# Sigmoid attention and a skip MoE: each block's kind read inside the block before, and the gathers' index tiles made one step earlier

## The chip, the core and the metric

The kernel runs on one core of a Trainium2 chip. A core has five engines with an instruction stream each: TensorE (PE in the profile; its weight loads are shown apart as PEld), VectorE (DVE), ScalarE (ACT), GpSimd (POOL) and SyncE (SP), which here issues transfers. An engine has a sequencer, which reads the stream, runs register operations, branches and waits itself, and hands the rest to the engine. The profile marks what a sequencer does with a q (PEldq, DVEq, ...). They meet only through semaphores. The metric is the device time of one execution in microseconds, lower is better.

## The reference

Inputs are `q`, `k`, `v` of shape (8, 12, 448, 64) and the weights of a mixture of 8 experts (768 to 1024 to 768), all float32.

```python
scores = scale * q @ k.T - log(448)
attn = sigmoid(scores)                      # no softmax: each weight by itself
x = (attn @ v) as 3584 rows of 768
do_compute = (x @ w_skip) > 0               # other rows pass through unchanged
e = argmax(x @ w_gate); gate = probability of e
out[row] = x[row] + gate * (relu(x[row] @ w1[e]) @ w2[e])
```

So each row that isn't skipped goes to one expert, and how many rows an expert gets is known only at run time.

## The kernel before

The attention takes the first part of the span (to about 284 us). It writes `x` to the output in DRAM, and for every row a record (gate, row number) to a list in DRAM, sorted by expert. The experts' weights are 6.3 MB each in float32, so they are streamed.

Two full blocks of 128 rows of the first expert are computed in straight code while the planner works out the rest: a table `slots` (line 1085) with three entries for each block that is to come. `HAS` says whether a further expert's weights are to be loaded, `NXT` which one, and `TYP` the kind of the block. Then a loop (line 1537) runs over the remaining blocks; its count is a register. In the profiled execution it turns 14 times. There are four kinds, each an arm of a nested branch (`choose`, line 1525; the branches are shown at lines 1526, 1527 and 1532):

- FULL (0) and SPLIT (3), both by `block`: 128 rows. A float32 product is made of three faster ones of high and low parts. SPLIT also takes the next expert's weights apart into such parts: high parts on ACT (`hi1`, `hi2`), low parts on DVE (`lo1`, `lo2`).
- HALF (2) and FEW (1): the remaining rows of an expert, at most 64 or 32 of them, multiplied with the raw float32 weights. The few rows leave most of PE's columns free, so two or four parts of a product run side by side. These arms also issue the loads of the next expert's weights on SP.

In the profiled execution a full-size block and a HALF or FEW block alternate: full, HALF, full, HALF, then full and FEW five times. The last FEW block ends the kernel.

Inside an arm the order of each engine's work is the order in the source (`manual_schedule` in `run`, line 1520). The parts that the change touches are:

- The loop's head, line 1538: `kind = entry(TYP, ds(i + 2, 1), mybir.ALL_ENGINES, SPLIT)`. All five engines load one word of `slots` from SBUF into a register (`entry`, line 1088; the loads appear at line 1089, as do the loads of `NXT` and `HAS` on SP). Then each engine branches by it. The limits given to a load are checked by a SEQ_ASSERT instruction.
- `fetch` (line 1262), once in each arm, behind the transposes `turn_x` (line 488, shown at 492) that empty `xn`. On POOL it touches `xn` and `rn`, makes the index tiles (`jk`, `ri`, `rx`, `rp[1]`, `rq`) from the record `rn` and the list of slots `rix`, and issues two gathers: the rows of the block after the next into `xn`, and the records of the one behind that into `rn`.
- `put` (line 1285), at the end of each arm. On POOL it copies the row numbers, waits for the finished rows (`seen`), copies them to `ys` in FULL and FEW arms, and scatters them with addition into the output.
- `shift` (line 1278): DVE moves the list `rix` on by one block, between `fetch` and `put`.
- `ready_x` (line 1105): ACT and DVE turn the transposed rows of the next block into `xh`, `xf` and `xl`. `take_rec`, `weigh_sum` and `advance` (DVE) handle the gates and row numbers.

In a FEW arm PE's order is: first layer (96 small matmuls into `ph`), transpose of the first half of the hidden rows (line 1412), `turn_x` (six transposes), transpose of the second half (line 1416), second layer (32 small matmuls into `py`). Both halves come from ACT (line 1408), and go back through ACT (line 1419).

Of the kernel before, what the change touches and what calls it, by code (L numbers as in the profile page):

```python
# [15 lines left out]
ALU = mybir.AluOpType  # L16
# [7 lines left out]
def kernel(  # L24
# [11 lines left out]
    nc = tc.nc  # L36
# [487 lines left out]
    def relu(h, hs, ph):  # L524
        nc.scalar.activation(hs[:, h * H1 : (h + 1) * H1], ph[h], AF.Relu)  # L525
# [683 lines left out]
    def next_expert(col):  # L1209
        return entry(NXT, col, SP, NE - 1), entry(HAS, col, SP, 1)  # L1210
# [30 lines left out]

    dve, pool = nc.vector, nc.gpsimd

    order.__exit__(None, None, None)
# [16 lines left out]

    def fetch():


        pool.tensor_tensor(xn[:, 0:1], xn[:, 0:1], zf, op=ALU.add)
        pool.tensor_tensor(jk, rn[:, 0:2], rn[:, 0:2], op=ALU.add)
        pool.tensor_copy(ri, rn[:, 1:2])
        pool.tensor_tensor(rn[:, 0:1], rn[:, 0:1], zf, op=ALU.add)
        pool.tensor_tensor(rx, rix[:, 5:6], zero, op=ALU.add)
        pool.tensor_tensor(rp[1], ri, zero, op=ALU.add)  # L1270
        pool.tensor_tensor(rq, rp[1], zero, op=ALU.add)
        got = gather(xn, rp[1])

        tc.declare_no_dep(got.ins, group="put", across_iterations=True, reason="a token is in one block only")
        tc.add_to_no_dep_group("got", got.ins)
        gather_rec(rn, rx)
# [8 lines left out]
    def put(n, last=None):  # L1285

        pool.tensor_tensor(rp[0], rid[:, 0:1], zero, op=ALU.add)
        pool.tensor_tensor(rs, rp[0], zero, op=ALU.add)
        if last is False:
            pool.drain()  # L1290
# [17 lines left out]
        tc.declare_no_dep(out_rows.ins, group="got", across_iterations=True, reason="a token is in one block only")  # L1308
        tc.add_to_no_dep_group("put", out_rows.ins)

    def advance(pieces=2):
# [15 lines left out]
    def block(i, last):  # L1327


        def split1(js, h):  # L1330
            if last:
                for j in js:
                    hi1(j, h)
                for j in js:
                    lo1(j, h)

        gemm1(0, range(G1), xh, xl, ph, last)
        relu(0, hs, ph)
# [6 lines left out]
        gemm1(1, range(9, G1), xh, xl, ph, last)  # L1345
        relu(1, hs, ph)
        for h in range(2):
            turn_x(xn, h, pxt[h])
        fetch()
        split1(range(3), 1)  # L1350
        gemm2(0, hh, hl, py)
# [3 lines left out]
        if last:  # L1355
            for h in range(2):
                whole_x(h, (slice(0, 3),))
            shift(dve)
        else:
            ready_x()  # L1360
        for j in range(1, NK2):
            gemm2(j, hh, hl, py)
# [11 lines left out]
        else:  # L1374
            shift(dve)
        for o in range(2):
            rows = ys if last else yt
            weigh_sum(rows[:, o * H2 : (o + 1) * H2], half_y(py, o), recs[:, 0, 0:1])
# [6 lines left out]
    def few(i):  # L1385

        nx = next_expert(ds(i + 2, 1))
        take_rec()

# [23 lines left out]
        for h in range(2):  # L1413
            turn_x(xn, h, pxt[h])
        fetch()
        nc.tensor.transpose(turned[1][:, :P], hs[:, parts[1]], ident)
        ht4 = ht[:, : 8 * SM].rearrange("p (c g t) -> p c g t", c=2, g=4)
        for s, p in zip(parts, turned):
            nc.scalar.activation(ht[:, s], p[:, :P], AF.Copy)
        ready_x()  # L1420
        shift(dve)

        for n, j in enumerate((0, 2, 1, 3)):
# [28 lines left out]
    def half(i):  # L1452

        nx = next_expert(ds(i + 2, 1))
        take_rec()

# [20 lines left out]
        for h in range(2):  # L1477
            turn_x(xn, h, pxt[h])
        fetch()
        for c in range(4):  # L1480
# [7 lines left out]
        ready_x()  # L1488
        shift(dve)

        ht8 = ht.rearrange("p (c h t) -> p c h t", c=4, h=2)
# [33 lines left out]
    def choose(kind, i):  # L1525
# [5 lines left out]
        with c.Else():  # L1531
            with tc.If(kind < SPLIT) as d:
                run(HALF, i)
            with d.Else():
                run(SPLIT, i)

    with tc.For_i(0, nreg, 1, iteration_sync="reg_based") as i:
        kind = entry(TYP, ds(i + 2, 1), mybir.ALL_ENGINES, SPLIT)
        choose(kind, i)
# [28 lines left out]
```

## Time and profile before

| | |
|---|---|
| median of 3 runs | 526.78 us (526.13 to 526.92) |
| the profiled execution's own time | 526.53 us |
| its span | 524.8 us |
| mean granted TensorE clock | 0.995 |
| busy share of the span: PE, DVE, ACT, POOL | 97%, 56%, 54%, 50% |
| loop, first matmul to the end of the span | 323.7 to 524.8 us |

How to read it: the span goes from the first to the last instruction of the program that the profile shows; the execution's own time has a little more around it. A row of instructions gives a line, an engine, an operation, what is written and read, and a count. In a timeline a row begins with the start and the duration in us, and brackets hold the engine's idle time before the instruction and what ended it; an idle time of POOL ahead of an operation that waits for a later engine costs nothing. Rows with three numbers between slashes give the shortest, the median and the longest duration in ns, then the first and last start in us. In the list of waits a row gives the total in us, how often, and the longest.

### The profile page before, as it was taken

What the parts mean: (1) busy time and instruction counts of PE and PEld (TensorE: products, weight loads), DVE (VectorE), ACT (ScalarE), POOL (GpSimd) and SP (SyncE); (2) the same over time, 40 slices, a digit from 0 to 9 for tenths busy, and PEclk for the clock granted to TensorE, in tenths of its full rate; (3) what the DMA queues carried; (4) which work ended last, traced back from release to release, by engine and by line L of the source; (5) the groups of instructions that cost most, each with busy time, mean ns of one, the idle gap of its engine ahead of it and who ended that gap; (6) DMA issues with size and microseconds to landing.
All of it is one profiled execution on the core that took longest, in us unless ns stands there. A gap on an engine that the chain in (4) does not pass through costs nothing.

```text
span 524.8 us, 15310 instructions
## 1 busy us (share of the span) xinstructions
PE 508.7 (97%) x5033; PEld 339.2 (65%) x5034; DVE 296.1 (56%) x721; ACT 281.0 (54%) x485; POOL 262.5 (50%) x414
## 2 busy tenths in 40 slices
PE   8999999999999999999989999999999999999991
PEld 7765555545545456555445989948669797978790
DVE  4556757648667676687684962862222322269422
ACT  5776776767767668677664211942112323268322
POOL 4523553443557666766574332553333645455644
PEclk9999999999999999999999999999999999999997
DMA  8999787898999999999955023979393959695942
GB/s 211 209 257 200 150 187 156 178 175 173 195 206 234 220 203 221 196 204 213 199 105 114 11 92 105 389 210 347 99 364 119 317 230 310 240 328 227 346 184 47
DMA packets 140288, 107.21 MB, mean 204 GB/s; under 512 B 97099, under 2 KB 112731, under 8 KB 140240
## 3 DMA queue, kind: packets, MB, share of 16 engines
q1 hardware_dynamic: 134000, 97.66, 70.0%
q0 software_dynamic: 4576, 8.65, 6.9%
q8 instruction: 30, 0.49, 0.4%
q10 hardware_dynamic: 1664, 0.26, 0.3%
q14 instruction: 18, 0.15, 0.1%
HBM read 98.49 MB, written 17.56 MB: 221 GB/s over the span
## 4 chain that ended last, share of the span: by engine, by line
PE 89%; DVE 3%; SPq 2%; DMA 2%; issue 1%; ACT 1%; POOL 0%; POOLq 0%; ACTq 0%; DVEq 0%
PE s L212 23%; PE pa L240 21%; PE ph L516 11%; PE py L544 11%; PE b_ph L516 3%; PE b_py L544 3%; PE ph L1391 3%; PE py L1458 2%; PE ph L1458 2%; PE pxt L492 2%; PE py L1391 2%; PE pl L280 1%; PE pht L530 1%; DMA out_dram<-y 1%; SPq L263 1%
## 5 line engine op out<-in xcount | busy, mean ns | idle before, releaser
L232 ACT ACTIVATE at<-s,bias 128x896 f32<-128x896 f32 (+1 forms) x191 | 173.3, 913 | 82.1 <-PE s L212 71.2
L212 PE MATMUL s<-x 64*64 64x448 f32 (+1 forms) x1528 | 165.4, 498 | 1.3 <-DVE wh L485 0.9
L240 PE MATMUL pa<-at,v 64*64 64x448 f32 (+1 forms) x1536 | 163.0, 489 | 0.0
L176 POOL COPY kq<-kq 32x896 f32<-32x896 f32 (+1 forms) x96 | 88.1, 917 | 94.6 <-DMA kq<-in_q_dram 59.0
L212 PEld LDWEIGHTS s<-x 64*64 64x64 f32 x1528 | 80.0, 191 | 53.1 <-issue 28.6
L240 PEld LDWEIGHTS pa<-at,v 64*64 64x64 f32 x1536 | 62.5, 133 | 54.9 <-issue 47.8
L194 DVE STREAM_TRANSPOSE x<-kq 128x448 f32<-128x448 f32 x94 | 80.8, 934 | 5.0 <-POOL kq L176 5.0
L250 DVE TENSOR_TENSOR xt<-xt,pa 128x448 f32<-128x448 f32 x48 | 29.7, 620 | 54.4 <-ACT xt L673 49.6
L414 POOL DMA_INDIRECT lst<-rec,idx x32 | 31.7, 989 | 17.4 <-DVE xt L250 5.8
L486 POOL TENSOR_TENSOR wl<-wr,wh 128x384 fp32r<-128x384 f32 (+1 forms) x28 | 31.2, 1125 | 12.6 <-DVE wh L485 8.1
L255 DVE STREAM_TRANSPOSE y<-xt 128x448 f32<-128x448 f32 x48 | 31.0, 645 | 6.8 <-DMA out_dram<-y 5.2
L574 POOL DMA_INDIRECT out_dram<-ys,rp x15 | 23.7, 1580 | 16.6 <-issue 8.4
L525 ACT ACTIVATE hs<-ph 128x512 f32<-128x512 f32 x14 | 8.3, 596 | 43.9 <-PE ph L516 37.5
L536 DVE TENSOR_TENSOR hl<-pht,hh 128x512 fp32r<-128x512 f32 x14 | 9.7, 690 | 36.5 <-ACT hh L535 22.8
L544 PE MATMUL py<-wh,hh 128*128 128x384 f32 x112 | 29.8, 347 | 0.0
L502 DVE TENSOR_TENSOR xl<-pxt,xh 128x384 fp32r<-128x384 f32 x30 | 15.3, 552 | 25.3 <-ACT xf L1097 17.8
L544 PE MATMUL py<-wh,hl 128*128 128x384 f32 x112 | 28.8, 338 | 0.0
L544 PE MATMUL py<-wl,hh 128*128 128x384 f32 x112 | 28.7, 337 | 0.0
L516 PE MATMUL ph<-wh,xh 128*128 128x512 f32 x84 | 25.7, 402 | 1.1 <-ACT yt L1444 0.8
L516 PE MATMUL ph<-wl,xh 128*128 128x512 f32 x84 | 26.6, 403 | 0.0
L673 ACT ACTIVATE xt<-pa 128x448 f32<-128x448 f32 x48 | 25.7, 536 | 0.8 <-PE pa L240 0.8
L516 PE MATMUL ph<-wh,xl 128*128 128x512 f32 x84 | 24.5, 395 | 0.0
(277 smaller groups left out, 686.4 us busy)
## 6 DMA issues: line engine op xcount, KB each, us to landing
raw<-in_moe_w_dram SPq DMA_DIRECT2D x64, 768.0 KB
v<-in_v_dram SPq DMA_DIRECT2D x48, 256.0 KB
out_dram<-y SPq DMA_DIRECT2D x192, 56.0 KB
kq<-in_k_dram SPq DMA_DIRECT2D x46, 224.0 KB
kq<-in_q_dram SPq DMA_DIRECT2D x46, 224.0 KB
wr<-in_moe_w_dram SPq DMA_DIRECT2D x12, 256.0 KB
wr<-in_moe_w_dram SPq DMA_DIRECT2D x16, 192.0 KB
lst<-fill SPq DMA_DIRECT2D x4, 464.0 KB
```

Of the source, the lines that this page charges most:

```text
L176: nc.gpsimd.tensor_copy(a[BT:, :, :, :BT], a[:BT, :, :, BT:])
L194: nc.vector.transpose(xs[:, n].rearrange("p (r j) -> p j r", j=NJ), t.rearrange("p (j d) -> p j d", d=D)[:, :, :BT],)
L212: nc.tensor.matmul(sc[m * D : (m + 1) * D, j, : qs.stop - qs.start], xs[r, 0, first::NR7], xs[r, 1, qs], start=True, stop=True,)
L232: nc.scalar.activation(at[:, :, :n], sc[:, :, :n], AF.Sigmoid, bias=bias, scale=SCALE)
L240: nc.tensor.matmul(pa[j * D : (j + 1) * D, r, qs], vt[rs, j, r + c if c < 3 else 3 * (1 - r), :], at[rs, j, : qs.stop - qs.start], start=( ...
L250: nc.vector.tensor_tensor(x, x, pa[:, 1, :S], op=ALU.add)
L255: nc.vector.transpose(y, xts[b][:, hp, :])
L414: put = nc.gpsimd.indirect_dma_start(out=lst[:, :], out_offset=bass.IndirectOffsetOnAxis(ap=idx[:, c : c + 1], axis=0), in_=rec[:, c, :], ...
L486: nc.gpsimd.tensor_tensor(lo, r, hi, op=ALU.subtract)
L516: nc.tensor.matmul(ph[h], a[:, j * P : (j + 1) * P], w[j][h], start=(n == 0), stop=(n == len(t) - 1),)
L544: last = nc.tensor.matmul(half_y(py, o), a[h][:, js], w[j][:, o * H2 : (o + 1) * H2], start=(j == 0 and n == 0), stop=(j == NK2 - 1 and n ...
L1391: nc.tensor.matmul(dst[g * SM : (g + 1) * SM, :n], a, w, start=(j == 0), stop=(j == most - 1), tile_position=(0, g * SM),)
```

## The change

The load of the kind leaves the loop's head. Five registers (`kinds`, one for each engine) are filled before the loop, and each arm loads the kind of the next block (`ds(i + 3, 1)`) into them, engine by engine, at places of its own. The loop's head only copies them into the value that the branches compare.

The five POOL operations that make the index tiles leave `fetch` and become `name_rows`. It is called once before the loop, and in `put`: behind the row numbers in FULL, SPLIT and HALF arms, behind the scatter in FEW arms. What remains of `fetch` touches `rn` first and then `xn`. In HALF arms POOL's load of the kind stands inside `fetch`.

```diff
+    ET = mybir.EngineType
+    kinds = nc.alloc_registers("kind", engines=mybir.ALL_ENGINES)
+
+    def next_kind(i, *engines):
+        for e in engines:
+            nc.engines[e].reg_mov(kinds[e], entry(TYP, ds(i + 3, 1), [e], SPLIT))
...
-    def fetch():
-        pool.tensor_tensor(xn[:, 0:1], xn[:, 0:1], zf, op=ALU.add)
+    def name_rows():
         pool.tensor_tensor(jk, rn[:, 0:2], rn[:, 0:2], op=ALU.add)
         pool.tensor_copy(ri, rn[:, 1:2])
-        pool.tensor_tensor(rn[:, 0:1], rn[:, 0:1], zf, op=ALU.add)
         pool.tensor_tensor(rx, rix[:, 5:6], zero, op=ALU.add)
         pool.tensor_tensor(rp[1], ri, zero, op=ALU.add)
         pool.tensor_tensor(rq, rp[1], zero, op=ALU.add)
+
+    def fetch(i=None):
+        pool.tensor_tensor(rn[:, 0:1], rn[:, 0:1], zf, op=ALU.add)
+        pool.tensor_tensor(xn[:, 0:1], xn[:, 0:1], zf, op=ALU.add)
+        if i is not None:
+            next_kind(i, ET.Pool)
         got = gather(xn, rp[1])
...
         pool.tensor_tensor(rp[0], rid[:, 0:1], zero, op=ALU.add)          # in put
         pool.tensor_tensor(rs, rp[0], zero, op=ALU.add)
+        if n != SM:
+            name_rows()
         if last is False:
             pool.drain()
...
         out_rows = scatter(rp[0][:n], ys[:n], ALU.add)
+        if n == SM:
+            name_rows()
...
+        next_kind(i, ET.SP)                       # block: ahead of the first layer
         gemm1(0, range(G1), xh, xl, ph, last)
...
         relu(1, hs, ph)
+        next_kind(i, ET.PE)
         for h in range(2):
             turn_x(xn, h, pxt[h])
         fetch()
+        next_kind(i, ET.Pool)
...
             shift(dve)                            # SPLIT
+            next_kind(i, ET.DVE)
         else:
             ready_x()
+        next_kind(i, ET.Activation)
...
             shift(dve)                            # FULL
+            next_kind(i, ET.DVE)
...
         nx = next_expert(ds(i + 2, 1))            # few
+        next_kind(i, ET.SP)
...
             turn_x(xn, h, pxt[h])
         fetch()
+        next_kind(i, ET.Pool)
+        next_kind(i, ET.PE)
         nc.tensor.transpose(turned[1][:, :P], hs[:, parts[1]], ident)
...
         shift(dve)
+        next_kind(i, ET.Activation, ET.DVE)
...
         nx = next_expert(ds(i + 2, 1))            # half
+        next_kind(i, ET.SP)
...
             turn_x(xn, h, pxt[h])
-        fetch()
+        fetch(i)
+        next_kind(i, ET.PE)
...
         shift(dve)
+        next_kind(i, ET.Activation, ET.DVE)
...
+    name_rows()
+    nc.regs_mov(kinds, entry(TYP, slice(2, 3), mybir.ALL_ENGINES, SPLIT))
     with tc.For_i(0, nreg, 1, iteration_sync="reg_based") as i:
-        kind = entry(TYP, ds(i + 2, 1), mybir.ALL_ENGINES, SPLIT)
+        kind = nc.snap(kinds, min_val=0, max_val=SPLIT)
         choose(kind, i)
```

## The prediction

> **What bounds the kernel now.** I read the page first, for the engine that sets the end.
>
> ```profile
> span 524.8 us, 15310 instructions
> ...
> PE 508.7 (97%) x5033; PEld 339.2 (65%) x5034; DVE 296.1 (56%) x721; ACT 281.0 (54%) x485; POOL 262.5 (50%) x414
> ```
>
> TensorE (PE) is busy for 97% of the span, so an edit on another engine pays only where PE waits for it. The change touches the expert loop alone, from about 323 us to the end. So next comes what PE waited for in the loop, then a table of the loop cut at PE's first matmul of each block (columns: window, its length, busy time of PE, PEld, DVE, ACT, POOL, clock, DMA), of which I show the four short FEW blocks that are followed by another block.
>
> ```profile
> PE ph L516 <- ACT yt L1444: 0.8, 1, 0.8
> PE ph L1391 <- ACT wh L1237: 0.3, 1, 0.3
> PE ph L516 <- issue: 0.3, 1, 0.3
> PE ph L1416 <- ACT hs L1408: 0.2, 1, 0.2
> ```
>
> ```profile
> 403.70:410.30 6.60, 6.60 (x138) 4.59 (x137) 2.19 (x9) 2.52 (x12) 3.95 (x12) 1.00 0.43 127
> 428.80:435.70 6.90, 6.67 (x137) 4.60 (x136) 2.46 (x10) 2.56 (x13) 4.26 (x12) 1.00 0.25 63
> 454.30:461.70 7.40, 6.65 (x137) 4.70 (x136) 2.94 (x11) 3.10 (x13) 4.80 (x12) 1.00 0.33 49
> 480.30:488.60 8.30, 7.66 (x137) 5.03 (x136) 7.31 (x16) 4.57 (x15) 4.50 (x10) 1.00 0.40 123
> ```
>
> In 200 us of loop PE idles 1.6 us in four places. Two of them are the first matmul (L516) of the block behind a FEW block, 0.3 and 0.8 us; those stages are 6.90 and 7.40 long where the undisturbed one has 6.60. That is the whole prize on PE. Are these two waits the load of the kind? The next rows are the loads (L1089 stands for the one at the loop's head and for those of the next expert), then PE's four loads inside FEW blocks, one window each. The three numbers are shortest, median and longest in ns.
>
> ```profile
> L1089 SPq FUSED_REGOPS  x42: 46/152/342, 335.1 to 516.7; - x42
> L1089 SPq SEQ_ASSERT  x28: 5/18/23, 335.4 to 516.9; - x28
> L1089 PEldq FUSED_REGOPS  x14: 51/51/56, 321.7 to 504.9; - x14
> L1089 PEldq TENSOR_LOAD <-slots x14: 302/310/1265, 321.9 to 505.0; - x14
> L1089 DVEq TENSOR_LOAD <-slots x14: 305/317/331, 324.9 to 509.7; - x14
> L1537 PEldq MOVE  x14: 29/37/43, 321.6 to 504.8; - x14
> ```
>
> ```profile
> L1089 PEldq TENSOR_LOAD <-slots x1: 459/459/459, 409.1 to 409.1; - x1
> L1089 PEldq TENSOR_LOAD <-slots x1: 972/972/972, 434.3 to 434.3; - x1
> L1089 PEldq TENSOR_LOAD <-slots x1: 1265/1265/1265, 459.7 to 459.7; - x1
> L1089 PEldq TENSOR_LOAD <-slots x1: 446/446/446, 487.1 to 487.1; - x1
> ```
>
> Yes. A load takes 0.31 us on PE, but 0.45 to 1.27 in the four that run while a FEW block's last matmuls stream, and PE idles behind exactly the two longest: the load at 434.3 ends at 435.3, the one at 459.7 at 461.0. The row that names ACT (L1444) is the profile's guess for the second.
>
> **The change, part by part.** *The load at the head goes, and a register move takes its place (0.04 us).* Where a FEW block ends this gives PE back 0.97 and 1.27 us of its sequencer, more than the idle time there, so both idles should close: -0.28 - 0.80 as the finer rows have them.
>
> ```profile
> 435.75 0.47 PE L516 MATMUL ph<-wh,xh 128*128 128x512 f32 x1 [0.28 <-issue]
> 461.75 0.47 PE L516 MATMUL ph<-wh,xh 128*128 128x512 f32 x1 [0.80 <-ACT yt L1444]
> ```
>
> That is **-1.08 us**; its bounds are 0 (the compares and semaphore waits behind the load hold PE instead) and 1.08 (a wait can't fall below zero). Behind full-size blocks the load is hidden already: it runs at 426.5, and the next block's first matmul is at 428.80, so the sequencer is 2.3 us ahead.
>
> ```profile
> L1089 PEldq TENSOR_LOAD <-slots x1: 302/302/302, 426.5 to 426.5; - x1
> 428.80 0.32 PE L1391 MATMUL ph<-raw,xf 128*32 128x128 f32 x4
> ```
>
> *PE's load moves into the arms.* In the full-size blocks it stands before the transposes of the next rows (L492), under that same lead: 0 (0.6 us a block without it). In HALF blocks it stands behind them, where PE's sequencer waits for ACT anyway, from 346.3 to 348.0: 0 too. In FEW blocks it stands behind the same six transposes and ahead of the second transpose of the hidden rows (L1416). The sequencer's rows there, and its next step (L1391):
>
> ```profile
> L1481 PEldq ALU_OP  x3: 32/32/32, 346.3 to 348.2; - x3
> L1481 PEldq EVENT_SEMAPHORE  x2: 51/51/51, 348.0 to 348.4; - x2
> ```
>
> ```profile
> L1416 PEldq ALU_OP  x1: 32/32/32, 406.4 to 406.4; - x1
> L1416 PEld LDWEIGHTS ph<-ident,hs x1: 141/141/141, 407.2 to 407.2; 128*128 128x128 f32 x1
> L1391 PEldq FUSED_REGOPS  x1: 37/37/37, 407.0 to 407.0; - x1
> ```
>
> The sequencer reaches L1416 at 406.4, waits there for ACT, and goes on at 407.0: 0.6 us of cover. The inserted steps are an address (0.05), the load (0.31) and a move (0.04); with some 0.07 us between steps, 0.6 us. Today only SP shows range checks (0.15 + 0.02, with gaps about 0.25), because one load serves all engines; a load for PE alone may carry its own check, which makes 0.85. The steps that feed the second layer's first matmul then come 0.1 us late (L1416's own issue, 0.1, falls behind the load) or 0.45 with a check. I can't tell which from this trace and take 0.25. It counts in the FEW blocks at 403.7, 428.8 and 454.3; the one at 480.3 waits for ACT at this place (the 0.2 us row of L1416), and the last one belongs to the tail. **+0.75 us**, bounds 0 and 1.35; if the load is as slow here as at its old place (mean of the four rows 0.79, 0.48 more), 2.8.
>
> The Trainium skill, "DMA: Bandwidth & Descriptors", section on latency and other measured facts, puts the floor of such a load at about 600 ns. The rows here say 0.31, and the measurement decides. By the page each of the three FEW blocks would lose 0.29 us more, and the sum would come out 0.9 us higher.
>
> *The other engines' loads.* ACT, DVE, SP and POOL load the same word in their arms; none of them is waited for by PE in the middle of a block, and each loses the same load at the head. They count only in the tail.
>
> *POOL's index tiles.* Five small operations (jk, ri, rx, rp, rq) go from the fetch into the store of the block before. In full-size blocks they now wait there for the record gather of the same block, with `drain`, the operation that looks at the finished rows, and the scatter queued behind them. POOL has room at that place:
>
> ```profile
> POOL jk L1293 <- DVE sv L1315: 41.0, 9, 5.6
> POOL xn L1265 <- PE pxt L492: 24.8, 7, 6.8
> POOL out_dram L574 <- POOLq L1537: 8.2, 1, 8.2
> ```
>
> It idles 41.0 us over nine blocks (4.6 each) before that operation, against less than 1 us for five steps. In FEW blocks they come behind the scatter, and the next fetch starts by waiting for PE's transposes anyway (24.8 us over seven). Before the loop POOL idles 8.2 us. So 0 in the middle of the run; the row gathers start about 0.85 us sooner and PE doesn't wait for them today. Were the cover gone, each block would pay about 0.9.
>
> *The tail.* Behind the last matmuls everything is on the path. POOL's steps, then DVE's:
>
> ```profile
> 511.89 0.28 POOL L1266 TENSOR_TENSOR jk<-rn 128x2 f32<-128x2 f32 x1
> ...
> 512.80 0.19 POOL L1271 TENSOR_TENSOR rq<-rp,zero 128x1 int32<-128x1 int32 x1
> 513.73 1.08 POOL L564 DMA_INDIRECT xn<-out_dram,rp  x1 [0.74 <-PE py L1391]
> ...
> 516.12 0.20 POOL L1287 TENSOR_TENSOR rp<-rid,zero 128x1 int32<-128x1 int32 x1
> ...
> 516.54 0.18 POOL L1293 TENSOR_TENSOR jk<-yt 32x2 f32<-32x2 f32 x1
> ...
> 518.65 1.41 POOL L574 DMA_INDIRECT out_dram<-ys,rp  x1 [0.62 <-issue]
> ```
>
> ```profile
> 514.58 0.21 DVE L1283 COPY rix<-riv 128x58 int32<-128x58 int32 x1
> 514.83 1.26 DVE L1446 SCALAR_TENSOR_TENSOR yt<-py,recs,yt 32x384 f32<-32x384 f32 x2
> ```
>
> Without the five steps (511.89 to 512.99, less the one for rn that stays, about 0.2) POOL's two gathers, and L1287 behind them, come 0.85 us sooner: 515.3. But DVE's load stands between rix and yt, where DVE is only 0.04 us idle: +0.6, or 0.85 with a check. The first half of yt is then ready at 516.1 to 516.35 instead of 515.45, and POOL looks at it (L1293) then instead of at 516.54: -0.45 to -0.2. If PE's late step in this FEW block delays ACT's copies by up to 0.3 us, DVE moves with them: +0.15 at worst. I take **-0.10**.
>
> **Sum:** -1.08 + 0.75 - 0.10 = -0.43 us. The profiled execution took 526.53 (span 524.8 and 1.7 around it), 0.25 below the median of 526.78, so the sum gives 526.10 on its own time and 526.35 against the median; I forecast **526.2**.
>
> **Rivals.** *Faster: the FEW loads hide wholly.* No check on PE, the wait for ACT covers all, and the tail gains its 0.45: -1.53, which is **525.1**. For it: the cover of 0.6 us equals the length of the steps. Against it: no margin, in three blocks.
>
> *Slower: PE's load stays slow in its new place.* It decides from the point where a FEW block loses 0.36 us (1.08 / 3): then the stall has only moved from the block's end to ahead of L1416. With the mean of the four slow rows and a check a FEW block loses 0.93: 2.79 - 1.08, and 0.3 in the tail as the DVE chain shifts, +2.0: **528.5**. For it: all four loads in FEW blocks were slow, while DVE's fourteen lie between 0.305 and 0.331. Against it: at the old place four small matmuls run at once, at the new one a single transpose, and beside the full-size matmuls the load took 0.30.
>
> The Trainium skill, "SBUF — State Buffer", section on the two separate sides, holds that engine reads and reads over the AXI ports can't slow each other. If so, the matmul stream isn't what slows these loads, and the "against" above falls; no row here shows what does.
>
> *The gain is lost again.* The FEW block at 480.3 takes 8.30 us instead of 6.60, since PE waits for ACT's copies of the next weights (L1237, 0.3 us and slack around it). If those copies follow the transfers and not PE, the 0.80 won at 461.7 ends there: -0.43 + 0.80, **526.9**.
>
> **How the numbers follow.** Chances: forecast 0.38, faster rival 0.32, slower rival 0.22, lost again 0.08. A measurement of this kernel tells 0.2%, 1.05 us, from no change. Faster takes nine tenths of its rival and 0.15 of the forecast's case (0.29 + 0.06 = 0.35); slower takes nine tenths of its rival and a twentieth of the rest (0.20 + 0.03 = 0.23); the rest, 0.42, is no change. The likeliest case alone spans 525.5 to 526.9; to hold eight in ten, the range goes from 524.9 (just past the faster rival) to 528.3 (most of the slower one).
>
> **What would show it.** Right: no idle time on PE ahead of L516 at the four ends of FEW blocks; PE's load in FEW blocks near 0.31 us, and L1416 or the second layer's first matmul 0.1 to 0.45 us later behind L492 than now; yt later behind rix, the last scatter a little sooner. Wrong: loads of half a microsecond or more in FEW blocks with PE idle ahead of L1416 or L1391; PE waiting for rows (L492); a scatter in full-size blocks that comes late and holds DVE; FEW stages that stay as long as today.

## The result, and where the time came from

The changed kernel is slower: 529.34 us in the median of 7 runs (528.03 to 531.95) against 524.31 us (524.05 to 526.92) for the kernel before. The ratio is 1.0084, with a 95% interval of 1.0057 to 1.0111. I had forecast 526.2 us and no change that can be measured, with 0.23 for slower. The seven runs of the kernel before fall into two groups: the three that were known when I predicted, 526.13 to 526.92 us, and four more at 524.05 to 524.31. So the base moved by some 2.5 us after the forecast, and against the first group alone the change costs 2.6 us instead of 5.0. On two more chips the unaltered change gave 1.0072 (1.0048 to 1.0096) and 1.0043 (1.0022 to 1.0063). Chips differ (the kernel before has medians from 524.3 to 527.8 us in these comparisons), so below a run is set only beside the kernel before on its own chip.

The page of the changed kernel says that PE is as busy as before, in a span that is 2.8 us longer:

```profile
span 527.6 us, 15599 instructions
...
PE 509.8 (97%) x5033; PEld 337.6 (64%) x5034; DVE 297.8 (56%) x721; ACT 282.1 (53%) x485; POOL 261.5 (50%) x419
```

The loop cut at PE's first matmul of each block shows where the 2.8 us are (lengths in us, from the two profiled executions):

| stage | before | after | difference |
|---|---|---|---|
| attention and routing, up to the loop's first matmul | 323.55 | 322.39 | -1.16 |
| first block of the loop | 18.60 | 19.08 | +0.48 |
| first three FEW blocks | 6.56, 6.95, 7.49 | 6.89, 6.88, 6.93 | -0.30 |
| SPLIT block | 18.52 | 18.58 | +0.06 |
| fourth FEW block | 8.36 | 10.51 | +2.15 |
| last FEW block, up to the first signal of the last barrier | 15.51 | 15.05 | -0.46 |
| the last barrier | 2.13 | 4.11 | +1.98 |
| the other seven blocks | 117.14 | 117.20 | +0.06 |

The first row says little of the change: the loop's first matmul starts anywhere from 322.3 to 325.5 us in the 18 profiles, at 322.3 to 324.1 in the three of the unaltered change.

The waits of PE in the loop of the changed kernel, and the four FEW blocks that another block follows (columns as in the prediction's table):

```profile
PE ph L1414 <- ACT wh L1237: 2.7, 4, 1.5
PE ph L516 <- DVEq L1568: 0.4, 1, 0.4
```

```profile
403.05:409.94 6.89, 6.83 (x137) 5.00 (x136) 2.90 (x11) 2.54 (x12) 4.16 (x7) 1.00 0.41 129
428.48:435.36 6.88, 6.88 (x138) 4.81 (x137) 2.88 (x11) 2.54 (x12) 4.01 (x12) 1.00 0.11 12
453.89:460.82 6.93, 6.92 (x138) 4.73 (x137) 3.42 (x11) 2.53 (x12) 3.96 (x11) 1.00 0.26 71
479.39:489.91 10.52, 7.78 (x138) 5.01 (x137) 8.95 (x18) 5.69 (x16) 4.81 (x10) 1.00 0.46 112
```

The waits ahead of L516 behind FEW blocks are gone, as foreseen. In their place PE waits 2.7 us for ACT's copies of weights (L1237) at the start of the fourth FEW block. The timeline of both engines there shows who is late:

```profile
477.77 1.58 ACT L1237 ACTIVATE wh<-raw 128x768 fp32r<-128x768 f32 x2
480.54 1.58 ACT L1237 ACTIVATE wh<-raw 128x768 fp32r<-128x768 f32 x2 [1.19 <-SPq L1561]
482.44 1.58 ACT L1237 ACTIVATE wh<-raw 128x768 fp32r<-128x768 f32 x2 [0.33 <-SPq L1561]
```

```profile
479.39 0.64 PE L1414 MATMUL ph<-raw,xf 128*32 128x128 f32 x16
481.53 0.43 PE L1414 MATMUL ph<-raw,xf 128*32 128x128 f32 x8 [1.49 <-ACT wh L1237]
```

ACT stops twice, since the last weights of the expert have not landed; in the kernel before it ran through its last six copies from 477.82 us on. So the late one is a transfer. When was it issued? These are SP's first transfers (L1213) in the second, third and fourth FEW block, first of the kernel before, then of the changed one:

```profile
433.08 0.71 SPq L1213 DMA_DIRECT2D raw<-in_moe_w_dram  x2
458.85 0.38 SPq L1213 DMA_DIRECT2D raw<-in_moe_w_dram  x1
483.79 0.38 SPq L1213 DMA_DIRECT2D raw<-in_moe_w_dram  x1
```

```profile
433.46 0.38 SPq L1213 DMA_DIRECT2D raw<-in_moe_w_dram  x1
459.99 0.38 SPq L1213 DMA_DIRECT2D raw<-in_moe_w_dram  x1
486.24 0.38 SPq L1213 DMA_DIRECT2D raw<-in_moe_w_dram  x1
```

Counted from the start of its block the issue stands at 4.27, 4.59 and 3.52 us before, and at 4.98, 6.10 and 6.85 after; the first FEW block, where nothing is late yet, has 2.4 in both. This is a chain of its own: eight transfers take 20 to 23.6 us, SP waits at the next arm's end until all have landed, then needs about 4.3 us to its next issue (branches, and three register loads with their checks). Together that is 25 to 28 us, while PE has done a full-size and a FEW block in 25.1. So from the second FEW block on the weights run on the edge, and what SP does between landing and issue counts.

But it is not SP that became slower by the change. These rows are its wait for the landing ahead of the third FEW block's issue, before and after, 0.5 us behind the last packet in both:

```profile
L1527 SPq EVENT_SEMAPHORE  x1: 17/17/17, 455.0 to 455.0; - x1
L1556 SPq EVENT_SEMAPHORE  x1: 17/17/17, 456.1 to 456.1; - x1
```

From there to the issue at 458.85 and 459.99 SP takes 3.8 us before and 3.9 us after, with three loads in both: the kernel before reads the kind in the same stretch, at the loop's head. What took longer are the transfers. From the first issue to the last packet the rounds of the first three FEW blocks took 21.9, 21.5 and 20.3 us before, and 23.6, 22.2 and 21.9 us after, together 4.0 us more; the steps between them were 0.85 us shorter. Why the transfers took longer isn't shown.

At the end, these rows give what the engines do in the last barrier of the changed kernel, and what the instruction queue moved from 524.1 to 527 us; the last row is the kernel before:

```profile
L1594 DVEq DRAIN  x1: 19/19/19, 524.1 to 524.1; - x1
L1594 ACTq DRAIN  x1: 141/141/141, 526.7 to 526.7; - x1
```

```profile
q14 instruction: 1, 0.01, 0.7%
```

```profile
L1563 ACTq DRAIN  x1: 14/14/14, 523.3 to 523.3; - x1
```

All engines pass a semaphore at 524.0. DVE drains 0.1 us later, ACT 2.7 us later, and in between, at 525.2, one 8 KB packet of program arrives. In the kernel before ACT drains 0.1 us behind its semaphore and no packet comes. The Trainium skill, "Runtime: NRT & Kernel Launch", section on instruction fetch mechanics, says that an engine's program is fetched in blocks by DMA, and that a branch out of the blocks at hand waits for one. The trace agrees as far as an engine that stands still around such a packet goes; whether a branch called for it no row shows. The packets of this queue have 8 KB, where the page has 16 KiB; those of the other instruction queue have 16.

At the loop's entry PE's second matmul waits for DVE, which reads the first kind as its last step before the loop:

```profile
322.39 0.40 PE L516 MATMUL ph<-wh,xh 128*128 128x512 f32 x1
323.18 0.50 PE L516 MATMUL ph<-wl,xh 128*128 128x512 f32 x1 [0.39 <-DVEq L1568]
```

So the theory to test has three losses: late weights (+2.15), a program fetch in the last barrier (+1.98), DVE's load ahead of the loop (+0.48).

### The profile page after: what moved, and what is told of

Read it like the earlier page. It is cut to its first block, busy times and chain, and to the rows that moved or that the text cites. A ratio compares the mean times of both kernels' runs of the same rounds, so it can differ in the third digit from the quotient of the medians.

```text
span 527.6 us, 15599 instructions
## 1 busy us (share of the span) xinstructions
PE 509.8 (97%) x5033; PEld 337.6 (64%) x5034; DVE 297.8 (56%) x721; ACT 282.1 (53%) x485; POOL 261.5 (50%) x419
## 5 line engine op out<-in xcount | busy, mean ns | idle before, releaser
L240 PEld LDWEIGHTS pa<-at,v 64*64 64x64 f32 x1536 | 61.4, 133 | 56.9 <-issue 50.2
L516 PE MATMUL ph<-wl,xh 128*128 128x512 f32 x84 | 26.6, 403 | 0.4 <-DVEq L1568 0.4
L516 PE MATMUL ph<-wh,xh 128*128 128x512 f32 x84 | 25.7, 403 | 0.0
L516 PE MATMUL ph<-wh,xl 128*128 128x512 f32 x84 | 24.5, 395 | 0.0
```

The source lines that it names most:

```text
L240: nc.tensor.matmul(pa[j * D : (j + 1) * D, r, qs], vt[rs, j, r + c if c < 3 else 3 * (1 - r), :], at[rs, j, : qs.stop - qs.start], start=( ...
L516: nc.tensor.matmul(ph[h], a[:, j * P : (j + 1) * P], w[j][h], start=(n == 0), stop=(n == len(t) - 1),)
```

## The experiments

Four groups of runs, each on one chip beside the kernel before. "Pair" is the SPLIT block with the fourth FEW block behind it, which takes 26.88 us in the profiled kernel before; "issue" the first transfer, in us behind the start of the second, third and fourth FEW block; "barrier" the step of the last barrier that is 0.94 us long without a fetch.

| run | median us | kernel before | ratio (95%) | pair | issue | barrier |
|---|---|---|---|---|---|---|
| kinds only | 530.59 | 527.71 | 1.0046 (1.0027 to 1.0066) | 29.71 | 4.9, 5.4, 6.2 | 2.8 |
| rows only | 527.01 | 527.71 | 0.9983 (0.9968 to 0.9998) | 27.17 | 2.5, 2.8, 3.5 | 0.9 |
| change, ACT 9 longer | 529.63 | 527.71 | 1.0045 (1.0024 to 1.0065) | 27.40 | 2.9, 4.2, 5.5 | 0.9 |
| change, SP late | 529.61 | 527.71 | 1.0042 (1.0029 to 1.0055) | 26.51 | 2.4, 2.4, 3.5 | 2.8 |
| change | 530.00 | 526.22 | 1.0072 (1.0048 to 1.0096) | 28.99 | 3.2, 5.7, 6.0 | 2.8 |
| change, both | 526.46 | 526.22 | 1.0015 (0.9996 to 1.0034) | 26.49 | 2.5, 2.4, 3.5 | 0.9 |
| before, SP's kind late | 525.95 | 526.22 | 0.9997 (0.9970 to 1.0024) | 26.25 | 2.9, 3.7, 3.5 | 0.9 |
| before, SP slower | 527.91 | 526.22 | 1.0040 (1.0020 to 1.0061) | 29.64 | 4.8, 7.3, 8.0 | 0.9 |
| before, SP all ahead | 527.13 | 525.34 | 1.0019 (1.0002 to 1.0037) | 27.02 | 2.4, 2.4, 3.5 | 0.9 |
| the same and rows | 527.22 | 525.34 | 1.0030 (1.0014 to 1.0046) | 26.93 | 2.4, 2.4, 3.5 | 0.9 |
| both, DVE early | 526.13 | 525.34 | 1.0013 (0.9996 to 1.0030) | 26.56 | 2.4, 2.4, 3.5 | 0.9 |
| both, without rows | 526.83 | 525.34 | 1.0032 (1.0015 to 1.0049) | 26.52 | 3.1, 3.5, 3.5 | 0.9 |
| change | 530.80 | 527.81 | 1.0043 (1.0022 to 1.0063) | 28.08 | 4.0, 4.5, 3.5 | 2.9 |
| change, ACT 3 longer | 529.26 | 527.81 | 1.0025 (1.0004 to 1.0045) | 27.40 | 3.5, 3.9, 3.5 | 0.9 |
| change, SP late | 529.96 | 527.81 | 1.0035 (1.0017 to 1.0053) | 26.51 | 2.4, 2.4, 3.5 | 2.8 |
| change, both | 527.51 | 527.81 | 0.9998 (0.9981 to 1.0015) | 26.49 | 2.4, 2.4, 3.5 | 0.9 |

### Which half of the change

The kinds alone: the index operations back in the fetch.

```diff
     def fetch(i=None):
...
+        pool.tensor_tensor(jk, rn[:, 0:2], rn[:, 0:2], op=ALU.add)
+        pool.tensor_copy(ri, rn[:, 1:2])
...
     def put(n, last=None):
...
-        if n != SM:
-            name_rows()
```

> The kind is read in the arms as in the changed kernel, the five index operations are back in the fetch. Theory A (the row gathers, which start 0.85 us sooner, take DMA time from the next expert's weights): the fourth FEW block, 10.5 us long in the changed kernel, goes back to about 8.4, and the time is about 2 us below the changed kernel's. Theory B (SP's own load and check of the kind, which now stand ahead of the weight transfers, make the weights late): the fourth FEW block stays at about 10.5 and the time within 0.5 us of the changed kernel's. Both: PE's second matmul of the loop still waits 0.4 us for DVE, and ScalarE's end of the program still comes 2 us late, since its program is as long as the changed kernel's.

The rows alone: the kernel before with `name_rows` called in `put` and once ahead of the loop; the kind is read at the loop's head.

> The index operations are made in the store as in the changed kernel, the kind is read at the loop's head by all engines as before. Theory A: the fourth FEW block takes about 10.5 us; with the tail's 0.4 us gained the time is 1.5 to 2 us above the kernel before. Theory B: it takes 8.0 to 8.6 and the time is 0 to 0.5 us below the kernel before. Both: no late instruction transfer at the end of the program, since ScalarE's program is as long as before; PE's waits of 0.28 and 0.80 us ahead of the blocks behind FEW blocks stay.

The loss belongs to the kinds: 1.0046 without the rows, with a long fourth FEW block (11.17 us) and the fetch. Theory A, that the earlier gathers crowd out the weights, falls: with the rows alone the weights come in time and the time is a little below the kernel before. That interval ends just under 1, so the 0.17% is barely more than nothing.

This run also bears on what makes a load of the kind slow. These are PE's loads at the ends of the same four FEW blocks as in the prediction, same instructions around them, in the run with the rows alone:

```profile
L1089 PEldq TENSOR_LOAD <-slots x1: 314/314/314, 410.4 to 410.4; - x1
L1089 PEldq TENSOR_LOAD <-slots x1: 302/302/302, 435.5 to 435.5; - x1
L1089 PEldq TENSOR_LOAD <-slots x1: 312/312/312, 460.6 to 460.6; - x1
L1089 PEldq TENSOR_LOAD <-slots x1: 303/303/303, 487.8 to 487.8; - x1
```

None is slow. PE's stream of matmuls by itself is not the cause, then.

### The two large losses mended, one at a time and together

The fetch: ACT loads the first block's kind three times more (later: once more) ahead of the loop, only to move the end of its program by nine (three) instructions.

```diff
+    for _ in range(3):
+        entry(TYP, slice(2, 3), [ET.Activation], SPLIT)
     nc.regs_mov(kinds, entry(TYP, slice(2, 3), mybir.ALL_ENGINES, SPLIT))
```

> The changed kernel with three more loads of the first block's kind by ScalarE ahead of the loop, where ScalarE has over 2 us to spare; they only make its program nine instructions longer. Theory C (the 2 us at the end are ScalarE's next piece of program, which it only fetches inside the last barrier): the fetch falls ahead of the barrier, the gap of 2.85 us in it goes back to about 0.9, and the time is 1.5 to 2 us below the changed kernel's. Rival (the end is late for what the operations behind the last scatter do): the gap stays and the time is within 0.5 us of the changed kernel's.

The weights: SP reads the kind behind the transfers, in FEW and HALF blocks.

```diff
         nx = next_expert(ds(i + 2, 1))
-        next_kind(i, ET.SP)
...
         for g in range(4):
             load_w2(g, nx)
+        next_kind(i, ET.SP)
```

> The changed kernel with SP's load of the kind behind the issue of the next expert's transfers in FEW and HALF blocks instead of ahead of them. Theory B (the chain landing, SP, issue, landing sets when ScalarE can round the weights): each FEW block issues 0.65 us sooner after the last landing, three rounds give about 2 us, the fourth FEW block takes about 8.5 us instead of 10.5, and the time is about 2 us below the changed kernel's. Theory A alone: the issue comes sooner but the block still takes over 10 us; under 0.7 us is gained.

Each did in the profile what it was made for: the barrier's step is back at 0.94 us in the one, the issues at 2.4 us and the fourth FEW block at 7.98 us in the other. In the first, a packet of program now came at the loop's entry (323.35 us), and the first block took 19.89 us instead of 19.1. The packet is not the reason: all six profiles with the longer program of ACT have it, and in four of them the block takes 18.95 to 19.10 us. Here ACT waits 1.9 us for weights that land late, as it does for 1.6 us in the run with the kinds alone, which has no such packet and a first block of 19.59 us. To know what the mends are worth in time, the unaltered change had to run beside them.

> The changed kernel once more, unaltered, so that the other runs can be set beside it on one chip. Both theories: about 0.8% above the kernel before; the fourth FEW block long (9 to 11 us) and the weight transfers of the FEW blocks issued 4 to 6 us after the block's start instead of 2.4.

> The changed kernel with SP's load of the kind behind the issue of the transfers in FEW and HALF blocks, and with one more load by ScalarE ahead of the loop, which makes its program three instructions longer. If the losses are the late weights and the program fetch in the last barrier, both go: transfers of the FEW blocks issued 2.4 to 3 us after the block's start, no gap of 2.85 us at the end, and 3 to 4 us less than the changed kernel; what is left against the kernel before is the 0.45 us that DVE's load costs at the loop's entry. Rival (the losses are noise of the two profiles): within 1 us of the changed kernel.

Both together, with only three instructions more on ACT, take 3.5 us off the changed kernel (530.00 to 526.46) and leave 0.15% that can't be told from nothing. The four cases on one chip divide the sum:

> The changed kernel unaltered, beside the next three on one chip: 0.7 to 0.85% above the kernel before, as in both comparisons so far.

> The changed kernel with one more load by ScalarE ahead of the loop, three instructions, and nothing else. If the fetch in the last barrier costs what its gap shows: 1.9 us (0.36%) less than the changed kernel unaltered, the fourth FEW block still long (9 to 11 us). If only the late weights count: no difference.

> The changed kernel with SP's load of the kind behind the transfers in FEW and HALF blocks, and nothing else. If the late weights count by themselves: 1.5 to 2 us (0.3 to 0.4%) less than the changed kernel unaltered, the fourth FEW block near 8.0 us, the gap of 2.85 us in the last barrier still there. If the long fourth FEW block was the luck of some profiles: within 0.5 us.

> Both edits, as in the mended kernel before. If the two losses add up: the sum of the two gains, 3.4 to 3.9 us less than the changed kernel unaltered and 0 to 0.3% above the kernel before. If one carries the whole: no better than that one alone.

The fetch mended alone gains 1.5 us, the weights alone 0.8, both 3.3. The single gains are below what I expected, and 0.8 us is not clear of the scatter (the runs of each kernel spread over 2.8 to 4.6 us here). Each is plainer on top of the other: the weights give 1.75 us where the fetch is mended (529.26 to 527.51), the fetch 2.45 where the weights are (529.96 to 527.51). So both count; that the two give 0.9 us more together than one by one is within the same scatter. The unaltered change stood 0.43% above the kernel before here, not at the 0.7 to 0.85% that I expected. The medians of the first group fit the same picture: each alone ends 0.42 to 0.45% above the kernel before, the change in the two later groups 0.43 to 0.72%. SP's first transfers in the run with its load late, and ACT in the barrier of the run with three more instructions:

```profile
432.22 0.38 SPq L1213 DMA_DIRECT2D raw<-in_moe_w_dram  x1
457.61 0.38 SPq L1213 DMA_DIRECT2D raw<-in_moe_w_dram  x1
484.18 0.38 SPq L1213 DMA_DIRECT2D raw<-in_moe_w_dram  x1
```

```profile
L1595 ACTq DRAIN  x2: 8/11/14, 525.1 to 526.1; - x2
```

Across all profiles the pair separates without overlap: 26.49 to 26.56 us in the six with SP's load of the change behind the transfers, 27.40 to 29.71 in the six with it ahead. Where in the pair it shows varies, and so it is not one loss. In the second profile of the unaltered change both blocks are long (19.29 and 9.70 us); in the third it is the SPLIT block alone (19.98 us), where PE waits for DVE, and DVE had been held by a late store of rows in the block before; its fourth FEW block is short (8.10 us). The profile with ACT three longer is like it (19.36 and 8.04). Long SPLIT blocks (19.3 to 19.5) stand also in three runs whose issues are early, the rows alone and both with SP all ahead, so this half of the excess isn't late weights, and why it is gone in all six with SP's load late (18.53 or 18.54) is open. The waits in the third profile:

```profile
DVE rid L1334 <- POOL rp L1299: 4.1, 1, 4.1
...
PE py L544 <- DVE hl L536: 1.2, 1, 1.2
```

### The chain of SP in the kernel before

First the kind alone, moved for SP alone; then the opposite, two more loads by SP ahead of the transfers.

```diff
-        kind = entry(TYP, ds(i + 2, 1), mybir.ALL_ENGINES, SPLIT)
+        now = entry(TYP, ds(i + 2, 1), others, SPLIT)
...
         for g in range(4):
             load_w2(g, nx)
+        sp_kind(i)
```

> The kernel before, with one edit: SP alone keeps the next block's kind in a register and reads it in the arms, in FEW and HALF blocks behind the transfers; all other engines read it at the loop's head as before, and the index operations stay in the fetch. If the chain from landing to issue to landing makes the weights late and brings the register loads into the start of the transfers: issues at 2.4 to 3 us after the FEW block's start, PE's loads at the ends of FEW blocks all near 0.31 us, FEW blocks of 6.6 us, the fourth under 8, and 1.5 to 2.5 us less than the kernel before. If PE's loads are slow because of its own matmul stream: they stay at 0.45 to 1.27 us and at most 0.5 us is gained.

```diff
     def few(i):
+        for _ in range(2):
+            entry(TYP, ds(i + 3, 1), SP, SPLIT)
         nx = next_expert(ds(i + 2, 1))
```

> The kernel before, with two more loads by SP ahead of the transfers in FEW blocks, some 1.3 us a block; nothing else is touched. If SP's time between landing and issue is on the path: the issue slips by about 1.3 us from FEW block to FEW block, the fourth FEW block takes 10 us or more, and the time is 2 to 4 us above the kernel before. If the transfers have slack: within 0.5 us of it.

The delay does what the chain says: the issue slips from block to block (4.8, 7.3, 8.0 us), the fourth FEW block takes 11.13 us, and the kernel loses 1.7 us, a little less than the 2 to 4 expected. The other direction was a miss: the weights came sooner (2.9, 3.7, 3.5), but the time did not change where I had expected 1.5 to 2.5 us, and one of PE's loads still took 1.03 us. I then took all three of SP's loads out of the way: `sp_next` reads the kind, the next expert and whether there is one, behind `load_w2`. One run was without and one with the rows in the store.

```diff
-        nx = next_expert(ds(i + 2, 1))
+        nx = nc.snap(nxs, min_val=0, max_val=NE - 1), nc.snap(has, min_val=0, max_val=1)
...
+        sp_next(ds(i + 3, 1))
```

> The kernel before, with SP's three loads for a block (the kind, the next expert, whether there is one) all read one block earlier, behind the issue of the transfers, and nothing else changed. If the chain from landing to issue sets the late weights: SP needs about 2 us less between the last landing and the next issue, the issues stand at 2.4 us after the start of each FEW block, FEW blocks take 6.6 us, the fourth 7.7, no load of PE is over 0.4 us, and the time is 1 to 2 us below the kernel before (0.2 to 0.4%). If the lateness comes from the transfers themselves: no change within 0.5 us, as with SP's kind alone.

> The run with all of SP's loads ahead, and the five index operations in the store as in the changed kernel. The index operations alone gave 0.17% on the kernel before. If the two gains add up: 0.3 to 0.5% below the kernel before, with the last scatter 0.4 us sooner behind the last block's start. If they are the same gain, weights that come in time: no better than the run with SP's loads alone.

In both, gains were expected (0.2 to 0.5%) and none came. The first three FEW blocks come within 0.03 us of the undisturbed one of the kernel before, 6.56 us, the fourth is with 7.67 us the shortest of all profiles (the four rows below, of the first of the two runs), no load of PE is over 0.33 us, and yet the kernels are 0.2 and 0.3% slower than before:

```profile
403.89:410.49 6.60, 6.60 (x138) 4.56 (x137) 2.74 (x10) 2.54 (x12) 3.88 (x11) 1.00 0.36 127
429.03:435.60 6.57, 6.57 (x137) 4.55 (x136) 2.74 (x10) 2.53 (x12) 3.88 (x11) 1.00 0.38 131
454.14:460.69 6.55, 6.55 (x137) 4.55 (x136) 2.73 (x10) 2.52 (x12) 3.88 (x11) 1.00 0.41 130
480.04:487.71 7.67, 7.27 (x137) 4.63 (x137) 7.45 (x13) 4.62 (x15) 3.39 (x4) 1.00 0.37 119
```

Its first block takes 19.59 us instead of 18.60. SP's loads ahead of the loop wait for the table `slots`, and the first transfers of the loop's first expert stand behind them: they are issued 10.7 us ahead of the loop's first matmul instead of 16.0. ACT gets its first weights late (ACT wh waits 2.1 us), and PE waits 0.4 us for ACT. The late issue doesn't explain it alone: with the rows in the store the issue is as late, ACT waits 1.3 us and the block takes 18.74 us. In the SPLIT block (19.35 us) PE waits 0.5 us for DVE. So of the 2.0 us that the four FEW blocks are shorter by, 1.0 and 0.8 went there in this profile. Apart from the rows alone, whose interval ends just under 1, no version here beats the kernel before by more than its measurement can tell.

### DVE's load ahead of the loop, and the rows once more

DVE reads the first kind right behind the table, not as its last step before the loop; everything else as in the mended kernel.

```diff
+    first_dve = entry(TYP, slice(2, 3), DV, SPLIT)
...
-    nc.regs_mov(kinds, entry(TYP, slice(2, 3), mybir.ALL_ENGINES, SPLIT))
+    first = entry(TYP, slice(2, 3), rest, SPLIT)
+    for x in rest:
+        nc.engines[x].reg_mov(kinds[x], first)
+    nc.vector.reg_mov(kinds[ET.DVE], first_dve)
```

> The mended kernel (SP's load behind the transfers, ScalarE's program three instructions longer) with DVE's first load of the kind right behind the table it reads, instead of as DVE's last step ahead of the loop. If that load is what PE waits for at the loop's entry: the first block takes 18.6 us instead of 19.09, PE's wait of 0.4 us at its second matmul goes, and the time is about 0.45 us below the mended kernel's, level with the kernel before. Rival (the wait comes with the register copy at the loop's entry): 19.09 stays.

PE's second matmul is no longer held, and the list of PE's waits in the loop is empty:

```profile
323.25 0.40 PE L516 MATMUL ph<-wh,xh 128*128 128x512 f32 x1
323.63 0.50 PE L516 MATMUL ph<-wl,xh 128*128 128x512 f32 x1
```

The offset against the kernel before falls from 0.49 to 0.10 us there, but 0.2 us come back at PE's transpose behind ACT (L530), and the block takes 18.95 us, not 18.6. In time, 1.0013 against 1.0015 of the mended kernel on another chip, this can't be seen.

> The mended kernel with the five index operations back in the fetch. If the index operations in the store are worth nothing of their own here: within 0.5 us of the mended kernel, the last scatter 0.4 us later behind the last block's start. If they cost by holding DVE in full-size blocks: up to 1 us faster than the mended kernel. If the gain of the rows alone is there on top of it: 0.5 to 1 us slower than the mended kernel.

Without the rows the mended kernel is 0.7 us slower in the median (526.83 against 526.13 of the run above, which also has DVE's load early, so 0.1 us of it may be that). The intervals overlap; the rows in the store are worth between nothing and 0.2%.

## Why the prediction was wrong, by its own steps

**The load at the loop's head, -1.08.** Right in what it does: no PE idle time ahead of L516 behind FEW blocks, in any profile with the kind in the arms. The size depends on the run, since the loads are slow only in some (below).

**PE's load inside FEW arms, +0.75.** Right, a little small. The loads carry their own check and take 0.30 to 0.33 us (at most 0.37 in the other runs with PE's load in the arms):

```profile
L1089 PEldq TENSOR_LOAD <-slots x14: 301/307/329, 328.4 to 511.2; - x14
L1089 PEldq SEQ_ASSERT  x14: 18/18/26, 329.1 to 511.9; - x14
```

The second layer's first matmul comes 0.16 us later than before in the first FEW block, the others up to 0.34, and the block grows from 6.56 to 6.89 us. Over three blocks +1.0 instead of +0.75, against -1.3 won behind the second and third (0.39 and 0.93): -0.3 net, as the table has it. The rival "stays slow in its new place", to which I gave 0.22 for slower, is refuted: the outcome was on its side, its mechanism was not there.

**"The other engines' loads" and its "none of them is waited for by PE in the middle of a block", the step that failed.** It gave these loads no term outside the tail, and three things were missed in it. First, ACT's load makes ACT's program longer, and with it the place moves at which a piece of program is fetched; the last barrier grew by 1.8 to 2.0 us in all six profiles with ACT's program at that length, and in none with three or nine instructions more. Second, DVE's load ahead of the loop is the last thing on which PE's second matmul depends, 0.4 to 0.5 us; of the time before the loop I looked at POOL alone. Third, SP's load stands ahead of eight transfers, in a chain that had no slack, and should have been priced by the weights and not by PE's waits. That SP loses the same load at the head was right (3.8 and 3.9 us of SP's time), so the load's own length doesn't account for the 2.15 us. What the runs show is the cure: with the load behind the transfers SP needs 3.2 us instead of 3.9 (without waits for free buffers), and the pair is short in all six profiles. That is less than the kernel before needs too, so it is no proof that the load made the weights late. The runs with both mended, level with the kernel before, show that the fetch and the late pair make up the measured loss; why the pair is late in the changed kernel stays open.

The rival "gain lost again" had the right place, the fourth FEW block behind ACT's copies, and the right releaser, the transfers. Its size was wrong by its assumption that the transfers keep their times: it could give back 0.80 us and no more, and the block lost 2.15. The transfers themselves took longer, 67.7 us over three rounds instead of 63.7.

**POOL's index tiles, 0.** About right in the sum: -0.17% by themselves. The new wait that I had listed, a late store in a full-size block that holds DVE, does occur: in the run with the rows alone PE waits 0.7 us for DVE in the SPLIT block. My reading of POOL's room was wrong. The 4.6 us of idle time a block would cover the five steps, but these can't start before the record gather has landed. The first row is the store ahead of the last FEW block in the kernel before, the others are of the second profile of the unaltered change:

```profile
508.32 0.19 POOL L1293 TENSOR_TENSOR jk<-yt 128x2 f32<-128x2 f32 x1 [5.62 <-DVE sv L1315]
508.60 0.19 POOL L1271 TENSOR_TENSOR jk<-rn 128x2 f32<-128x2 f32 x1 [3.61 <-DMA rn<-lst,rx]
510.76 0.20 POOL L1307 TENSOR_TENSOR jk<-yt 128x2 f32<-128x2 f32 x1 [1.22 <-DVE rid L1334]
518.25 0.21 POOL L1299 TENSOR_TENSOR rp<-rid,zero 128x1 int32<-128x1 int32 x1 [0.45 <-DMA out_dram<-ys,rp]
```

Counted from the last block's first matmul POOL looks at the finished rows at 1.15 us before, and at 2.49 there.

**The tail, -0.10.** The last scatter starts 11.07 us behind the block's first matmul instead of 11.48. That is 0.41 sooner, within the bounds and better than the value taken, but it is luck of this profile. In the other eleven with the rows in the store it starts at 11.64 to 12.67 us, 12.54 and 11.89 in the later two of the unaltered change; in the six without, at 11.48 to 11.75. So the term has the wrong sign: the store ahead of the last block comes late, and POOL's row numbers (L1299, the last row above) then wait in most of these profiles for that store's scatter to land. The sum had neither wait. In the 12.54 a load of DVE also took 1.0 us just ahead of its last steps. And where I had expected the last run, without the rows, to scatter 0.4 us later, it does so 0.4 us sooner than the run beside it (11.54 and 11.97).

**The rivals' times.** From the base that gives 526.2, the +2.0 of the slower rival is 528.7 and not 528.5, and the +0.37 of the lost gain 527.0 and not 526.9. Neither changes the argument.

**The explanation of the slow loads** ("while a FEW block's last matmuls stream") was wrong. The same stream of matmuls stood beside loads of 0.30 us in the run with the rows alone and of 1.26 us in the kernel before. The Trainium skill, "SBUF — State Buffer", section on the two separate sides, holds that engine reads and reads over the AXI ports can't slow each other. As far as PE's reads go, these rows agree, if the register loads use those ports, which no run here shows.

## What to carry to other kernels

Before moving a step between engines or places, ask of each queue what stands behind it, and add up every chain that paces itself: here landing, SP, issue, landing took as long as the work that it fed, so 1.3 us more of SP's time a round, on an engine that looks idle, cost 0.40% of the whole. Instructions that cost nothing where they run still lengthen a program, and a fetch of program in the wrong place, 2 us inside a barrier, can cost more than the edit could win; look at the instruction queue and the last barrier in each trace before reading a difference of 0.4%. When an edit is spread over five engines, price each engine's share by itself: moving one load of SP and adding three instructions to ACT took the measured loss away. And a cure is not yet a cause: count the same stretch in the kernel before, too.

## What the runs showed that I had not expected

A register load of 0.26 to 0.33 us can take much longer on any engine, up to 1.27 us on PE and DVE and up to 0.87 on POOL. The 51 loads of over 0.4 us in the 18 profiles, among some 1600 in and just ahead of the loop, all overlap a gather or scatter of POOL or begin within 2.4 us of its end. An example from the changed kernel, DVE's load and POOL's gather:

```profile
L1089 DVEq TENSOR_LOAD <-slots x1: 1265/1265/1265, 461.1 to 461.1; - x1
```

```profile
461.38 1.05 POOL L564 DMA_INDIRECT xn<-out_dram,rp  x1 [0.83 <-PE ph L516]
```

Of all these loads over 1000 are that near, and most of them are not slow, so nearness alone does not make one. What does was not tried.

The transfers of a round also vary. From its first issue to its last packet the round that starts in the first FEW block takes 20.9 to 22.6 us in 16 profiles, and 23.3 and 23.6 in those of the kinds alone and of the changed kernel; in the second profile of the unaltered change the next round takes 23.6. In all three profiles of the unaltered change one issue of SP in that first round, usually 0.37 us, took 2.3 to 2.6 us, in the others at most 1.75; but the three rounds are not all long (23.6, 21.8, 22.6), so that is no explanation. Over three rounds the six profiles with SP's load of the change ahead of the transfers have 64.5 to 67.7 us, the six with it behind 63.5 to 65.7, the kernel before 63.7 and the rows alone 63.0. Whether the load's place brings the long rounds about stays open; the kernel before with 1.3 us of loads more in that place shows the slip without them (19.9 to 22.0).
